# Holding back K matmuls behind the modulation columns, and moving one quarter's scale columns ahead of a chunk's K

## The chip, the cores and the metric

The kernel runs on one core of one Trainium2 chip. The metric is device time in microseconds (us).

## The reference, cut to what matters

```python
x = A_x                                               # (1, 2048, 1024), bf16
mod = (silu(c) @ w_mod).reshape(1, 6, 1, -1)          # w_mod: (1024, 6144)
sa, ca, ga, sb, cb, gb = (mod[:, i] for i in range(6))
h = layernorm(x) * (1 + ca) + sa                      # ca: scale, sa: shift
qkv = h @ A_wqkv                                      # then linear attention with phi(q), phi(k)
x = x + ga * (attention(qkv) @ A_wo)
h = layernorm(x) * (1 + cb) + sb
x = x + gb * ((gelu(h @ B_w_gate) * (h @ B_w_up)) @ B_w_down)
```

Only the start matters here: the scale `1 + ca` and the shift `sa` have to be computed from `c` before any projection of `h` can run.

## The kernel before

Every operation is recorded into one in-order stream for each engine, with semaphore waits worked out from the bytes it reads and writes. TensorE therefore executes its matmuls in the order in which the Python code records them, as the timelines below show.

The first stage works on the first four chunks (128 rows each) of x. A chunk is normalized, transposed on TensorE, copied to `h1T` by ScalarE, and scaled and shifted there by VectorE. The 1024 channels are eight blocks `dc` of 128. A "quarter" q covers `dc` 2q and 2q+1: its modulation values come from 32 small matmuls with one column each, 16 for the shift (`t=0`) and 16 for the scale (`t=1`). VectorE copies them out of PSUM, then scales `h1T`, and only then the K matmuls on these blocks may run.

```python
def wmq_dma(q, ts=(0, 1)):                  # weights of one quarter's columns: shift half first
    for t in ts:
        sch.dma(Q, ... WMQ[q][:, :, t, :] <- w_mod ...)
...
x_dma(0, 1); x_dma(1, 2)
wmq_dma(0, (1,))                            # first quarter: scale half first
x_dma(2, 3)
wmq_dma(0, (0,))
x_dma(3, 4)
w_dma(WK, OFF_WK, "wk", 1, 0, D, 0, 2)      # K weights of dc 0, 1
for q in range(1, 4):
    wmq_dma(q)
    ...                                     # K weights of dc 2q, 2q+1
...                                         # wv, x chunks 4 to 7, wq
```

```python
def mod_cols(q, bank):                      # 32 matmuls 128x1
    for t in range(2):
        for b in range(2):
            for dc in range(NDC): ...       # waits for r_wmq(q, t)

def k_part(q, cs):                          # K matmuls of quarter q for the chunks cs
    for dc in (2 * q, 2 * q + 1):
        for (c_, jg), b in kb0.items():     # seven PSUM banks; chunk 3's second half has bank 4
            if c_ in cs:
                kv_mm(c_, "k", jg, b, [dc])
        if 3 in cs:
            k31([dc])
```

`warm(n)` records n matmuls on zeros, to keep TensorE busy while it would wait. The order of the first stage is in the diff below. After it come V of the four chunks, then the rest of the kernel.

Of the kernel before, what the change touches and what calls it, by code (L numbers as in the profile page):

```python
# [17 lines left out]
NDC = D // P  # L18
# [196 lines left out]
def bass_adaLN_cond__linear_attn_block__geglu_ffn__prompt_kernel(  # L215
# [15 lines left out]
    with ExitStack() as es:  # L231
# [85 lines left out]
        def r_sm(name):  # L317
            return [(SMO[name], SMO[name] + SMSZ[name], name)]
# [13 lines left out]
        def r_h1(sg, k0=0, k1=NDC, s0=0, s1=SGW):  # L332
            return r_t8(H1O[sg], f"h1T{sg}", k0, k1, s0, s1)
# [7 lines left out]
        def r_w(off, name, dc, c0=0, c1=D):  # L341
            return [(off + (dc * D + c0) * 2, off + (dc * D + c1) * 2, name)]
# [14 lines left out]
        def r_wmq(i, t):  # L357
            return [(MSO[i] + (dc * 2 + t) * 512, MSO[i] + (dc * 2 + t + 1) * 512, f"wmq{i}") for dc in range(NDC)]
# [33 lines left out]
        def pr(b):  # L392
            return [(b * 2048, (b + 1) * 2048)]

        def PS(b, c0=0, c1=512):
            return ps_all[:, b * 512 + c0: b * 512 + c1]
# [17 lines left out]
        def pset_writer(b, o):  # L414
            for t_ in pr(b):
                sch.ps.set_writer(t_[0], t_[1], o)
# [87 lines left out]
        def xhat_dve(c_, dst, rng):  # L504
            sch.op(V, lambda e: e.tensor_scalar(dst[:, :], XALL[:, c_, :], MVA[:, c_, 0:1], RSA[:, c_:c_ + 1],
                                                op0=ALU.subtract, op1=ALU.mult),
                   rd=r_x(c_) + r_smc("mv", c_, 8) + r_smc("rs", c_, 4), wr=rng, note=f"xhat {c_}")
# [21 lines left out]
        def xh_buf(c_):  # L529
            i = c_ % 3  # L530
            return XH[i], r_2k(XHO[i], f"xh{i}")
# [52 lines left out]
        def mod1(c0, n, dc0=0, dc1=NDC):  # L584
            sg, ci = divmod(c0, CPG)
            mods(H1, r_h1, sg, sc1, ci * P, (ci + n) * P, dc0, dc1, "h1")
# [5 lines left out]

        MC0 = 496

        def mod_cols(q, bank):
            o = None
            rng = [(bank * 2048 + (MC0 + q * 4) * 4, bank * 2048 + (MC0 + q * 4 + 4) * 4)]
            for t in range(2):
                for b in range(2):
                    col = MC0 + q * 4 + t * 2 + b  # L600
                    for dc in range(NDC):
                        o = sch.op(T, lambda e, t=t, b=b, dc=dc, col=col: e.matmul(  # L602
                            PS(bank, col, col + 1), WMQ[q][:, dc, t, b * P:(b + 1) * P], SILUT[:, dc:dc + 1],
                            start=(q == t == b == dc == 0), stop=(dc == NDC - 1), skip_group_check=True),
                            rd=r_wmq(q, t) + r_sm("siluT"), pwr=(rng if dc == 0 else ()), note=f"mod{q}.{t}.{b}.{dc}")
            for t_ in rng:
                sch.ps.set_writer(t_[0], t_[1], o)

        def mod_copy(q, bank):
            rng = [(bank * 2048 + (MC0 + q * 4) * 4, bank * 2048 + (MC0 + q * 4 + 4) * 4)]  # L610
            sch.op(V, lambda e: e.tensor_tensor(MODT[:, q * 4:q * 4 + 4], PS(bank, MC0 + q * 4, MC0 + q * 4 + 4), ADD4[:, :], ALU.add),
                   prd=rng, rd=r_sm("add4"), wr=r_smc("modt", q, 16), note=f"modcp{q}")
# [62 lines left out]
        def kv_mm(c_, kind, jg, bank, dcs):  # L675
            sg, ci = divmod(c_, CPG)
            W_, off, name = (WK, OFF_WK, "wk") if kind == "k" else (WV, OFF_WV, "wv")
            o = None
            for dc in dcs:
                o = sch.op(T, lambda e, dc=dc: e.matmul(PS(bank), H1[sg][:, dc, ci * P:(ci + 1) * P], W_[:, dc, jg * 512:(jg + 1) * 512],  # L680
                                                        start=(dc == 0), stop=(dc == NDC - 1)),
                           rd=r_h1(sg, dc, dc + 1, ci * P, (ci + 1) * P) + r_w(off, name, dc, jg * 512, (jg + 1) * 512),
                           pwr=(pr(bank) if dc == 0 else ()), note=f"{kind} c{c_} jg{jg} dc{dc}")
            if dcs[-1] == NDC - 1:
                pset_writer(bank, o)
# [26 lines left out]
        def nb():  # L712
            b = bank_i[0] % bank_i[1]
            bank_i[0] += 1
            return b
# [18 lines left out]
        def warm(n, bank=None):  # L734
            for _ in range(n):
                sch.op(T, lambda e: e.matmul(PS(0 if bank is None else bank), WARM[:, 0:P], WARM[:, :], start=bank is not None,
                                             stop=bank is not None, skip_group_check=True),
                       rd=R_WARM, pwr=pr(bank) if bank is not None else (), note="warm")
# [12 lines left out]
        kb0 = {(0, 0): 0, (0, 1): 1, (1, 0): 2, (1, 1): 3, (2, 0): 5, (2, 1): 6, (3, 0): 7}  # L751

        def k31(dcs, c0=0, c1=MC0):
            rng = [(4 * 2048 + c0 * 4, 4 * 2048 + c1 * 4)]
            for dc in dcs:
                o = sch.op(T, lambda e, dc=dc: e.matmul(PS(4, c0, c1), H1[0][:, dc, 3 * P:4 * P], WK[:, dc, 512 + c0:512 + c1],  # L756
                                                        start=(c0 > 0 and dc == 0), stop=(dc == NDC - 1), skip_group_check=True),
                           rd=r_h1(0, dc, dc + 1, 3 * P, 4 * P) + r_w(OFF_WK, "wk", dc, 512 + c0, 512 + c1),
                           pwr=(rng if dc == 0 else ()), note=f"k c3 jg1 dc{dc} {c0}")
            if dcs[-1] == NDC - 1:  # L760
                sch.ps.set_writer(*rng[0], o)

        def k_part(q, cs):
            for dc in (2 * q, 2 * q + 1):
                for (c_, jg), b in kb0.items():
# [4 lines that stand above are left out]
# [10 lines left out]
        ln1_fin(1)  # L780
        warm(6, 7)
        mod_cols(0, 4)
        ln1_bn(2, 0)
        xhat_dve(1, *xh_buf(1))
# [4 lines left out]
        mod1(0, 1, 0, 2)  # L789
        warm(4, 7)  # L790
        k_part(0, [0])
        xhat_dve(2, *xh_buf(2))
        t1(2, 7)
        mod1(1, 1, 0, 2)
        ln1_bn(3, 0)
        ln1_bn(3, 1)
        ln1_fin(3)
        k_part(0, [1])
        mod1(2, 1, 0, 2)
        warm(2)  # L800
        k_part(0, [2])
        xhat_dve(3, *xh_buf(3))
        mod_cols(1, 4)
        mod_copy(1, 4)
        t1(3, 7)
        mod1(0, 3, 2, 4)
        k_part(1, [0, 1, 2])
        mod1(3, 1, 0, 4)
        k_part(0, [3])
        k_part(1, [3])  # L810
        mod_cols(2, 4)
        mod_copy(2, 4)
        warm(2)
        mod1(0, 1, 4, 5)
        mod1(1, 3, 4, 5)
        mod1(0, 4, 5, 6)
        k_part(2, [0, 1, 2])
        mod_cols(3, 4)
        mod_copy(3, 4)
        mod1(0, 1, 6, 8)  # L820
        mod1(1, 3, 6, 8)
        for dc in (4, 5):
            kv_mm(3, "k", 0, kb0[3, 0], [dc])
        for (c_, jg), b in kb0.items():
            kv_mm(c_, "k", jg, b, [6, 7])
        k31([4, 5, 6, 7])
# [4 lines left out]
        for c_ in range(4):  # L831
            for vc, jg in (((0, 0), (1, 0)), ((0, 1), (1, 1)), ((2, 0), (2, 1)), ((3, 0), (3, 1)))[c_]:
                b = nb()
# [58 lines left out]
        for c_ in range(4, NCH):  # L892
# [23 lines left out]
            for jg in range(2):  # L916
                b = nb()
# [3 lines left out]
            for jg in range(2):  # L921
                b = nb()
# [386 lines left out]
```

## Time and profile before

| | before |
|---|---|
| time, median of the first 3 runs | 838.55 us (838.42 to 838.92) |
| span of the profiled run | 836.7 us |
| TensorE busy | 830.1 us, 99% |
| TensorE's waits in the first 70 us | 4.2 us |
| first V matmul starts | 31.53 us |

First, from the page of the kernel before, the busy time of each engine and the chain of work that ended last. TensorE is the limit nearly everywhere.

```profile
PE 830.1 (99%) x4194; PEld 384.4 (46%) x4194; DVE 512.2 (61%) x898; ACT 336.4 (40%) x555; POOL 37.4 (4%) x91
PE 98%; DMA 1%; DVE 0%; SPq 0%; ACT 0%; issue 0%
```

The list of who waited for whom (TensorE, first 70 us): how long in total, how many times, the longest. L478 is the transpose of c, L602 the modulation columns, L680 the K and V matmuls, L565 VectorE's scaling of h1T; further down, L546 is the transposes of a chunk and L756 the K matmuls of chunk 3's second half.

```profile
PE ps_all L478 <- DMA c<-in_c_dram: 2.4, 1, 2.4
PE ps_all L602 <- DMA wmq<-in_w_mod_dram: 1.1, 1, 1.1
PE ps_all L680 <- DVE h1T L565: 0.7, 4, 0.2
```

The four short waits understate what is lost there, because warm-up matmuls (L736) fill part of each. This is seen in the timeline of TensorE, kernel before. Its columns are start, length to the end of the last instruction's pipeline, what, and in brackets the idle time before it and what ended it.

```profile
13.33 1.03 PE L680 MATMUL ps_all<-wk,h1T 128*128 128x512 bf16 x4
14.20 0.59 PE L736 MATMUL ps_all<-warm 128*128 128x512 bf16 x2
14.96 1.04 PE L680 MATMUL ps_all<-wk,h1T 128*128 128x512 bf16 x4 [0.17 <-DVE h1T L565]
15.84 0.94 PE L602 MATMUL ps_all<-siluT,wmq 128*128 128x1 bf16 x32
...
21.75 0.94 PE L602 MATMUL ps_all<-siluT,wmq 128*128 128x1 bf16 x32
22.55 0.59 PE L736 MATMUL ps_all<-warm 128*128 128x512 bf16 x2
23.30 2.76 PE L680 MATMUL ps_all<-wk,h1T 128*128 128x512 bf16 x12 [0.15 <-DVE h1T L565]
25.90 0.94 PE L602 MATMUL ps_all<-siluT,wmq 128*128 128x1 bf16 x32
26.70 0.59 PE L680 MATMUL ps_all<-wk,h1T 128*128 128x512 bf16 x2
27.45 3.20 PE L680 MATMUL ps_all<-wk,h1T 128*128 128x512 bf16 x14 [0.15 <-DVE h1T L565]
30.49 1.18 PE L756 MATMUL ps_all<-wk,h1T 128*128 128x496 bf16 x12
31.53 0.59 PE L680 MATMUL ps_all<-wv,h1T 128*128 128x512 bf16 x2
```

Start to start, the 12 K matmuls from 23.30 to 25.90 take 2.60 us, 0.216 us each; 32 columns take 0.80 us, 0.025 us each. The stretches that end at 14.96, 23.30 and 27.45 us are the targets of the change. From 22.55 to 23.30 us nothing useful ran (0.75 us); from 26.70 to 27.45 us two K matmuls did.

A reading that no printed line gives: the time at which a transfer landed. A transfer raises its semaphore in 16 steps, and the trace records the time of each. The Trainium skill, page "DMA: Bandwidth & Descriptors", section "Why a DMA increments its semaphore by 16 and not by 1", says that up to 16 engines finish independently and that only the full 16 means that all data landed. The second quarter's scale half, in the kernel before: its sixteenth step came at 15.46 us. All landing times below are sixteenth steps. The shift half, issued before it, landed at 13.68 us.

### The profile page before, as it was taken

What the parts mean: (1) busy time and instruction counts of PE and PEld (TensorE: products, weight loads), DVE (VectorE), ACT (ScalarE), POOL (GpSimd) and SP (SyncE); (2) the same over time, 40 slices, a digit from 0 to 9 for tenths busy, and PEclk for the clock granted to TensorE, in tenths of its full rate; (3) what the DMA queues carried; (4) which work ended last, traced back from release to release, by engine and by line L of the source; (5) the groups of instructions that cost most, each with busy time, mean ns of one, the idle gap of its engine ahead of it and who ended that gap; (6) DMA issues with size and microseconds to landing.
All of it is one profiled execution on the core that took longest, in us unless ns stands there. A gap on an engine that the chain in (4) does not pass through costs nothing.

```text
span 836.7 us, 11362 instructions
## 1 busy us (share of the span) xinstructions
PE 830.1 (99%) x4194; PEld 384.4 (46%) x4194; DVE 512.2 (61%) x898; ACT 336.4 (40%) x555; POOL 37.4 (4%) x91
## 2 busy tenths in 40 slices
PE   8999999999999999999999999999999999999998
PEld 4444444444444444444444444444444444444445
DVE  6678877687785577753455665356556535655512
ACT  2357777446423355420354442045554104445300
POOL 2012111000200000010000000000000000000000
DMA  9984422239696779180555533055553305555000
GB/s 288 318 250 104 99 76 76 77 80 235 139 237 203 225 203 275 29 194 26 158 151 151 152 101 76 19 158 152 151 151 101 76 20 159 153 154 144 7 19 26
DMA packets 184102, 113.22 MB, mean 135 GB/s; under 512 B 35560, under 2 KB 175080, under 8 KB 183024
## 3 DMA queue, kind: packets, MB, share of 16 engines
q1 hardware_dynamic: 184032, 112.50, 49.8%
q8 instruction: 33, 0.54, 0.3%
q14 instruction: 21, 0.17, 0.1%
q10 hardware_dynamic: 16, 0.00, 0.0%
HBM read 100.67 MB, written 4.47 MB: 126 GB/s over the span
## 4 chain that ended last, share of the span: by engine, by line
PE 98%; DMA 1%; DVE 0%; SPq 0%; ACT 0%; issue 0%
PE ps_all L1149 23%; PE ps_all L1121 23%; PE ps_all L1124 23%; PE ps_all L680 13%; PE ps_all L1064 7%; PE ps_all L721 7%; PE ps_all L702 1%; DMA wmq<-in_w_mod_dram 1%; PE ps_all L966 0%; PE ps_all L602 0%; PE ps_all L978 0%; PE ps_all L756 0%; PE ps_all L643 0%; SPq L442 0%; DVE h1T L565 0%; ACT h1T L548 0%
## 5 line engine op out<-in xcount | busy, mean ns | idle before, releaser
L1121 PE MATMUL ps_all<-h2T,wg 128*128 128x512 bf16 x896 | 339.6, 379 | 0.0
L1124 PE MATMUL ps_all<-h2T,wu 128*128 128x512 bf16 x896 | 339.6, 379 | 0.0
L1149 PE MATMUL ps_all<-wd,yT 128*128 128x512 bf16 (+3 forms) x952 | 194.2, 366 | 0.0
L1132 ACT ACTIVATE q<-ps_all 128x512 f32<-128x512 f32 x112 | 66.9, 597 | 225.3 <-PE ps_all L1121 221.5
L1149 PEld LDWEIGHTS ps_all<-wd,yT 128*128 128x128 bf16 x952 | 90.1, 98 | 103.9 <-issue 0.4
L1121 PEld LDWEIGHTS ps_all<-h2T,wg 128*128 128x128 bf16 x896 | 87.7, 98 | 105.8 <-issue 0.2
L1124 PEld LDWEIGHTS ps_all<-h2T,wu 128*128 128x128 bf16 x896 | 87.7, 98 | 105.6
L1137 DVE SCALAR_TENSOR_TENSOR ww<-th,guh 128x512 f32<-128x512 f32 x112 | 77.5, 692 | 77.9 <-ACT th L1136 77.9
L1134 DVE SCALAR_TENSOR_TENSOR ww<-q,ps_all 128x512 f32<-128x512 f32 x112 | 76.9, 687 | 77.5 <-ACT guh L1133 77.5
L1136 ACT ACTIVATE th<-ww 128x512 f32<-128x512 f32 x112 | 70.5, 629 | 87.4 <-DVE ww L1134 87.4
L1154 DVE TENSOR_TENSOR ps_all<-ps_all,gbb 128x512 f32<-128x512 f32 (+3 forms) x34 | 22.7, 667 | 94.8 <-PE ps_all L1149 94.8
L1139 DVE TENSOR_TENSOR yT<-ww,ps_all 128x512 bf16<-128x512 f32 x112 | 76.9, 686 | 3.8
L1133 ACT ACTIVATE guh<-ps_all 128x512 f32<-128x512 f32 x112 | 66.2, 591 | 0.0
L721 PE MATMUL ps_all<-h1T,wq 128*128 128x512 bf16 x256 | 58.7, 379 | 0.0
L680 PE MATMUL ps_all<-wk,h1T 128*128 128x512 bf16 x248 | 57.2, 379 | 0.7 <-DVE h1T L565 0.7
L680 PE MATMUL ps_all<-wv,h1T 128*128 128x512 bf16 x256 | 57.7, 379 | 0.0
L669 ACT ACTIVATE eb<-ps_all 128x512 f32<-128x512 f32 x64 | 37.5, 599 | 49.4 <-PE ps_all L721 21.8
L1064 PE MATMUL ps_all<-w,pq 128*128 128x512 bf16 x256 | 56.2, 379 | 0.0
L670 DVE TENSOR_SCALAR eb<-eb 128x512 f32<-128x512 f32 x64 | 27.1, 423 | 26.0 <-ACT eb L669 25.7
L1064 PEld LDWEIGHTS ps_all<-w,pq 128*128 128x128 bf16 x256 | 25.0, 98 | 30.2 <-issue 0.2
L680 PEld LDWEIGHTS ps_all<-wv,h1T 128*128 128x128 bf16 x256 | 24.9, 98 | 29.5
L680 PEld LDWEIGHTS ps_all<-wk,h1T 128*128 128x128 bf16 x248 | 23.7, 98 | 30.1 <-DVE h1T L565 2.9
(96 smaller groups left out, 481.7 us busy)
## 6 DMA issues: line engine op xcount, KB each, us to landing
wg<-in_B_w_gate_dram SPq DMA_DIRECT2D x56, 512.0 KB, 4.1
wu<-in_B_w_up_dram SPq DMA_DIRECT2D x56, 512.0 KB, 5.3
rb<-scr_rd SPq DMA_DIRECT2D x32, 256.0 KB, 6.7
wd<-in_B_w_down_dram SPq DMA_DIRECT2D x7, 1024.0 KB, 9.3
wmst<-in_w_mod_dram SPq DMA_DIRECT2D x6, 1024.0 KB, 6.9
wmq<-in_w_mod_dram SPq DMA_DIRECT2D x8, 512.0 KB, 6.9
out_dram<-xall SPq DMA_DIRECT2D x31, 128.0 KB, 1.7
xall<-in_A_x_dram SPq DMA_DIRECT2D x3, 1024.0 KB, 12.2
```

The lines of the kernel that those rows point to most:

```text
L680: o = sch.op(T, lambda e, dc=dc: e.matmul(PS(bank), H1[sg][:, dc, ci * P:(ci + 1) * P], W_[:, dc, jg * 512:(jg + 1) * 512], start=(dc == 0 ...
L721: o = sch.op(T, lambda e, dc=dc: e.matmul(PS(b), WQ[:, dc, qc * P:(qc + 1) * P], H1[sg][:, dc, :], start=(dc == 0), stop=(dc == NDC - 1)), ...
L1064: last[half] = sch.op(T, lambda e, g=g, half=half: e.matmul(PS(b0 + half), PQ[sg][:, g, ci * P:(ci + 1) * P], W2[:, g, half * 512:(half + ...
L1121: og = sch.op(T, lambda e, dc=dc: e.matmul(PS(bg), WG[slot][:, dc, e_ * P:(e_ + 1) * P], H2[sg][:, dc, :], start=(dc == 0), stop=(dc == ND ...
L1124: ou = sch.op(T, lambda e, dc=dc: e.matmul(PS(bu), WU[slot][:, dc, e_ * P:(e_ + 1) * P], H2[sg][:, dc, :], start=(dc == 0), stop=(dc == ND ...
L1132: sch.op(A, lambda e: e.activation(Q1[j][:, :], PS(bg), ACTF.Square, scale=math.sqrt(GELU_A)), prd=pr(bg), wr=rq, note=f"q1 {fc}")
L1133: ogh = sch.op(A, lambda e: e.activation(GUH[j][:, :], PS(bg), ACTF.Copy, scale=0.5), prd=pr(bg), wr=rg, note=f"gh {fc}")
L1134: sch.op(V, lambda e: e.scalar_tensor_tensor(WW[j][:, :], Q1[j][:, :], 1.0, PS(bg), op0=ALU.add, op1=ALU.mult), rd=rq, prd=pr(bg), wr=rw, ...
L1136: sch.op(A, lambda e: e.activation(TH[j][:, :], WW[j][:, :], ACTF.Tanh, scale=GELU_C), rd=rw, wr=rt, note=f"th {fc}")
L1137: sch.op(V, lambda e: e.scalar_tensor_tensor(WW[j][:, :], TH[j][:, :], 1.0, GUH[j][:, :], op0=ALU.add, op1=ALU.mult), rd=rt + rg, wr=rw, n ...
L1139: sch.op(V, lambda e: e.tensor_tensor(YT[:, fc, :], WW[j][:, :], PS(bu), ALU.mult), rd=rw, prd=pr(bu), wr=r_yt(fc), note=f"yT {fc}")
L1149: o = sch.op(T, lambda e, b=b, fc=fc, c0=c0, c1=c1, n=n: e.matmul(PS(b, 0, n), YT[:, fc, ci * P:(ci + 1) * P], WDT[fc // 4][:, fc % 4, c0:c1],
```

## The change

Its intent: fill the stretches in which TensorE waits for VectorE with real work. Four K matmuls of chunks 2 and 3 are held back and recorded behind the third quarter's columns, and four (two more than before) behind the fourth's. For the second quarter the 16 scale columns go ahead of chunk 2's K, in place of a warm-up pair. Columns now run scale first by default, in every quarter; the order of the transfers is not changed.

```diff
--- before.py
+++ after.py
@@ -592,16 +592,16 @@
 
         MC0 = 496
 
-        def mod_cols(q, bank):
+        def mod_cols(q, bank, ts=(1, 0)):
             o = None
             rng = [(bank * 2048 + (MC0 + q * 4) * 4, bank * 2048 + (MC0 + q * 4 + 4) * 4)]
-            for t in range(2):
+            for t in ts:
                 for b in range(2):
                     col = MC0 + q * 4 + t * 2 + b
                     for dc in range(NDC):
                         o = sch.op(T, lambda e, t=t, b=b, dc=dc, col=col: e.matmul(
                             PS(bank, col, col + 1), WMQ[q][:, dc, t, b * P:(b + 1) * P], SILUT[:, dc:dc + 1],
-                            start=(q == t == b == dc == 0), stop=(dc == NDC - 1), skip_group_check=True),
+                            start=(q == b == dc == 0 and t == 1), stop=(dc == NDC - 1), skip_group_check=True),
                             rd=r_wmq(q, t) + r_sm("siluT"), pwr=(rng if dc == 0 else ()), note=f"mod{q}.{t}.{b}.{dc}")
             for t_ in rng:
                 sch.ps.set_writer(t_[0], t_[1], o)
@@ -759,6 +759,11 @@
                            pwr=(rng if dc == 0 else ()), note=f"k c3 jg1 dc{dc} {c0}")
             if dcs[-1] == NDC - 1:
                 sch.ps.set_writer(*rng[0], o)
+
+        def k_tiles(dcs, tiles):
+            for dc in dcs:
+                for c_, jg in tiles:
+                    kv_mm(c_, "k", jg, kb0[c_, jg], [dc])
 
         def k_part(q, cs):
             for dc in (2 * q, 2 * q + 1):
@@ -797,30 +802,33 @@
         ln1_fin(3)
         k_part(0, [1])
         mod1(2, 1, 0, 2)
-        warm(2)
+        mod_cols(1, 4, (1,))
         k_part(0, [2])
         xhat_dve(3, *xh_buf(3))
-        mod_cols(1, 4)
+        mod_cols(1, 4, (0,))
         mod_copy(1, 4)
         t1(3, 7)
         mod1(0, 3, 2, 4)
-        k_part(1, [0, 1, 2])
+        k_tiles([2, 3], [(0, 0), (0, 1), (1, 0), (1, 1)])
+        k_tiles([2], [(2, 0), (2, 1)])
         mod1(3, 1, 0, 4)
         k_part(0, [3])
-        k_part(1, [3])
+        k31([2, 3])
         mod_cols(2, 4)
         mod_copy(2, 4)
-        warm(2)
+        k_tiles([3], [(2, 0), (2, 1)])
+        k_tiles([2, 3], [(3, 0)])
         mod1(0, 1, 4, 5)
         mod1(1, 3, 4, 5)
         mod1(0, 4, 5, 6)
-        k_part(2, [0, 1, 2])
+        k_tiles([4, 5], [(0, 0), (0, 1), (1, 0), (1, 1)])
+        k_tiles([4], [(2, 0), (2, 1)])
         mod_cols(3, 4)
         mod_copy(3, 4)
         mod1(0, 1, 6, 8)
         mod1(1, 3, 6, 8)
-        for dc in (4, 5):
-            kv_mm(3, "k", 0, kb0[3, 0], [dc])
+        k_tiles([5], [(2, 0), (2, 1)])
+        k_tiles([4, 5], [(3, 0)])
         for (c_, jg), b in kb0.items():
             kv_mm(c_, "k", jg, b, [6, 7])
         k31([4, 5, 6, 7])
```

## The prediction

> **What bounds the kernel now.** The page gives a span of 836.7 us with TensorE busy 99%; the chain of waits runs 98% through TensorE. Its waits in the list lie in the first 28 us: 2.4 us for c, 1.1 us for the first modulation weights, four of 0.15 to 0.20 us for VectorE's h1T scaling. From the last K block at 27.45 us on, the timeline shows matmuls without a gap, so what the first V matmul (31.53 us) gains, the span gains, if later transfers are in time.
>
> **Durations in the trace.** A 128x512 matmul issues every 0.216 us, a modulation column matmul every 0.025 us (32 take 0.80 us). The Trainium skill, page "TensorE: Matmul & The Clock Gate", section "Wait — 56ns, not 53.3ns?", states N/2.4 + 2.5 ns and a floor near 25 ns; the trace agrees. After a quarter's columns VectorE takes a copy (0.16 us) and a scaling (0.31 to 0.38 us) before the next K matmul: 0.75 to 0.81 us on TensorE.
>
> **What the change does, on the chain.**
> - Warm-up: two pairs go (0.43 us each). Each only filled a wait; alone that gains nothing.
> - Third quarter: before, 22.55 to 23.30 us (0.75 us) held no useful matmul. Now four held-back K matmuls (0.86 us) fill it: gain 0.75 us.
> - Fourth quarter: 26.70 to 27.45 us held two K matmuls (0.43 us); now four: gain 0.32 us.
> - First quarter, scale columns first: those weights landed at 6.3 us, so 16 columns run before the shift weights land (9.80 us): 0.40 us earlier. But the first K block needs wk's first part, landed at 11.89 us by its semaphore's increments, and K started at 12.03: the gain is lost there.
> - Second quarter: the scale columns move from 15.8 us to 14.2 us, ahead of chunk 2's K. The queue loads the shift half first (landed 13.68 us), the scale half second: 15.46 us by its last increment. TensorE takes its work in order, so it stalls from 14.2 to about 15.5 us, when chunk 2's K could have run at 14.96. Then 16 columns (0.40), four K (0.87), 16 columns (0.40) end at about 17.2 us against 16.64: cost 0.54 us.
>
> Later transfers are in time by this count: wk 2-3 16.86 (needed 18.0), third quarter's columns 20.40 (21.4), fourth's 24.60 (25.25), wk 7 25.99 (26.9), wv 27.67 (31.0).
>
> **Sum** (an estimate from these durations): +0.54 - 0.75 - 0.32 = about -0.5 us.
>
> **Prediction:** 838.0 us; 8 in 10 between 837.2 and 838.7. Faster by over 2%: 0.003; within 2%: 0.994; slower by over 2%: 0.003.
>
> **What the profile should show.** A new TensorE wait of about 1.3 us for wmq near 14.2 us; chunk 2's K near 15.9 us rather than 14.96; the first V near 31.0 us; the 0.15 us waits behind the third and fourth quarters' columns gone; the first K still near 12.0 us; everything after 31 us as before, some 0.5 us earlier; wmq and wk landing as before.
>
> **What would make it wrong.** If the scale half lands by 14.2 us in unprofiled runs, the cost vanishes and up to 1.1 us is gained, limited then by the fourth quarter's columns at 24.60 us. If transfers land later, or the idle stretch lowers the TensorE clock, the gain shrinks or becomes a loss. If the span does not follow the first V matmul, some later transfer or VectorE work binds at a fixed time. Noise of a few tenths of a us is of the effect's own size.

## The result, and the profile after

| | before | after |
|---|---|---|
| median | 839.04 us (6 runs, 838.42 to 840.65) | 838.45 us (6 runs, 838.12 to 839.1) |
| ratio of fast runs, 95% interval | | 0.9992 [0.9979, 1.0005] |
| span of the profiled run | 836.7 us | 836.2 us |
| first V matmul starts | 31.53 us | 31.00 us |
| from there to the end | 805.21 us | 805.22 us |

A ratio is the mean time of one kernel's fast runs over that of the other's of the same rounds, so it is not quite the ratio of the medians. The interval includes 1: these times alone do not show this change. (Pooled with the round of after_again below, 15 runs of before have a mean of 838.98 us and 11 of the change 838.49 us, 0.49 us apart; their ranges overlap.) Where time is gained and lost is read from the traces. From the first V matmul to the end it is 805.21 or 805.22 us in all thirteen profiled executions, whatever the kernel, so the start of the first V matmul carries the whole difference between them.

The list of TensorE's waits after the change, first 70 us:

```profile
PE ps_all L478 <- POOL bmask L429: 2.1, 1, 2.1
PE ps_all L602 <- DMA wmq<-in_w_mod_dram: 1.9, 2, 1.0
PE ps_all L680 <- DMA wk<-in_A_wqkv_dram: 0.4, 1, 0.4
PE ps_all L680 <- DVE h1T L565: 0.2, 1, 0.2
```

Three of the four waits for VectorE's scaling are gone, and a second wait for `wmq`, of 1.0 us, is new. The timeline of TensorE after the change shows both:

```profile
13.52 1.03 PE L680 MATMUL ps_all<-wk,h1T 128*128 128x512 bf16 x4
15.52 0.55 PE L602 MATMUL ps_all<-siluT,wmq 128*128 128x1 bf16 x16 [0.98 <-DMA wmq<-in_w_mod_dram]
15.94 1.02 PE L680 MATMUL ps_all<-wk,h1T 128*128 128x512 bf16 x4
16.80 0.54 PE L602 MATMUL ps_all<-siluT,wmq 128*128 128x1 bf16 x16
...
21.45 0.94 PE L602 MATMUL ps_all<-siluT,wmq 128*128 128x1 bf16 x32
22.25 3.18 PE L680 MATMUL ps_all<-wk,h1T 128*128 128x512 bf16 x14
25.27 0.94 PE L602 MATMUL ps_all<-siluT,wmq 128*128 128x1 bf16 x32
26.08 4.04 PE L680 MATMUL ps_all<-wk,h1T 128*128 128x512 bf16 x18
29.96 1.19 PE L756 MATMUL ps_all<-wk,h1T 128*128 128x496 bf16 x12
31.00 1.02 PE L680 MATMUL ps_all<-wv,h1T 128*128 128x512 bf16 x4
```

Behind the third and fourth quarter's columns K now runs on without a gap (14 and 18 matmuls in a row). Where the warm-up pair was, TensorE stands still until 15.52 us: the four K matmuls from 13.52 us, 0.216 us each, filled the time to 14.38. The chain of work after the change puts a transfer at that place:

```profile
7.17 8.31 DMA wmq<-in_w_mod_dram
15.48 0.05 issue
15.52 0.55 PE ps_all L602 x16
16.08 0.89 PE ps_all L680 x4
```

The transfer ends at 15.48 us, the sixteenth step of the scale half; the shift half had landed at 13.84 us. Chunk 2's first scaled block was ready at 15.09 us on VectorE, and its weights had landed at 12.07 us, so its K could have run about 0.8 us before it did.

### The profile page after: what moved, and what is told of

It is laid out like the page before. It is cut to its first block, busy times and chain, and to the rows that moved or that the text cites. A ratio compares the mean times of both kernels' runs of the same rounds, so it can differ in the third digit from the quotient of the medians.

```text
span 836.2 us, 11354 instructions
## 1 busy us (share of the span) xinstructions
PE 829.1 (99%) x4190; PEld 384.3 (46%) x4190; DVE 512.3 (61%) x898; ACT 336.3 (40%) x555; POOL 37.5 (4%) x91
## 4 chain that ended last, share of the span: by engine, by line
PE 98%; DMA 1%; SPq 1%; DVE 0%; issue 0%
PE ps_all L1157 23%; PE ps_all L1132 23%; PE ps_all L1129 23%; PE ps_all L680 13%; PE ps_all L1072 7%; PE ps_all L721 7%; DMA wmq<-in_w_mod_dram 1%; PE ps_all L702 1%; SPq L442 0%; PE ps_all L974 0%; PE ps_all L602 0%; PE ps_all L986 0%; PE ps_all L756 0%; SPq L453 0%; PE ps_all L643 0%
```

## The experiments

The theory: (a) the held-back K fills the two later stretches, worth about 1.07 us; (b) the early scale columns wait for weights that the queue loads second, which costs about 0.54 us; (c) the first quarter's order and the warm-up pairs are worth nothing. Rivals: splitting the columns costs by itself; the gain comes from the warm-up pairs or the first quarter; the transfers limit the stage altogether, so that a removed wait returns elsewhere.

How to read them. The landing of one and the same transfer moves by up to 1.6 us between executions (wk's first part, 11.28 to 12.88 us in the eleven traces that load it at the same place). The first K starts 0.13 to 0.14 us behind that landing in most traces. So the first V alone does not compare two kernels: before, e5 and e6 all took 19.50 or 19.51 us from the first K to the first V, but had the first V at 31.53, 31.80 and 31.09 us. Both the first V and the distance from the first K to it are given. The readings of all profiled executions, in us:

| kernel | wk's first part landed | first K | chunk 2's K | first V | first K to first V |
|---|---|---|---|---|---|
| before | 11.89 | 12.03 | 14.96 | 31.53 | 19.50 |
| after | 12.07 | 12.21 | 15.94 | 31.00 | 18.79 |
| e1_shift_first | 11.55 | 11.69 | 14.62 | 30.93 | 19.24 |
| e2_scale_loaded_first | 12.88 | 13.02 | 15.96 | 31.03 | 18.01 |
| e3_hold_back_only | 12.22 | 12.36 | 15.29 | 31.02 | 18.66 |
| e4_scale_early_only | 12.33 | 12.46 | 16.22 | 32.37 | 19.91 |
| e2_again | 12.32 | 12.46 | 15.39 | 31.26 | 18.80 |
| e5_first_quarter_scale_first | 12.16 | 12.29 | 15.23 | 31.80 | 19.51 |
| e6_no_warm_pairs | 11.45 | 11.59 | 14.52 | 31.09 | 19.50 |
| e7_best | 11.02 | 11.45 | 14.39 | 30.84 | 19.39 |
| after_again | 11.28 | 11.41 | 15.30 | 30.88 | 19.47 |
| e1_again | 12.13 | 12.27 | 15.20 | 30.45 | 18.18 |
| e7_again | 10.65 | 11.03 | 13.97 | 30.13 | 19.10 |

All kernels gave correct results. The profiled runs are of the fast state, except those of e5 and e6, which ran once and have the state unknown; the granted clock was 1.00 in all.

### e1_shift_first and e1_again: the other half of the columns first

```diff
 # in the changed kernel
-        mod_cols(1, 4, (1,))
+        mod_cols(1, 4, (0,))
         k_part(0, [2])
         xhat_dve(3, *xh_buf(3))
-        mod_cols(1, 4, (0,))
+        mod_cols(1, 4, (1,))
```

> The changed kernel with one edit: of the second quarter's columns the shift half, whose weights land first (13.7 us), goes ahead of chunk 2's K, and the scale half behind it. If the 1.0 us wait at 14.5 us is the landing of the scale half's weights at 15.48 us (theory), it goes: the early columns run at 14.4, chunk 2's K start near 15.1 us on VectorE's scaling, the scale columns near 16.0, and the first V matmul comes at 30.3 us instead of 31.0 (before: 31.53); 0.7 us less than the change, 1.2 us less than before, ratio to before 0.9985. The fourth quarter's columns then come up against their landing at 24.5 us, a wait of at most 0.1 us. If splitting the columns around K is itself what costs (rival), the first V matmul stays at 31.0 us.

Measured: 837.92 us (5 runs, 837.74 to 838.44), ratio to before 0.9988 [0.9975, 1.0]. The early columns ran at 13.86 us (planned about 14.4; this execution's first K was half a us earlier), without a wait. But the first V came at 30.93 us, not 30.3. The timeline of TensorE in this run shows where the gain went:

```profile
20.99 0.95 PE L602 MATMUL ps_all<-siluT,wmq 128*128 128x1 bf16 x32 [0.68 <-DMA wmq<-in_w_mod_dram]
21.81 3.18 PE L680 MATMUL ps_all<-wk,h1T 128*128 128x512 bf16 x14
25.20 0.95 PE L602 MATMUL ps_all<-siluT,wmq 128*128 128x1 bf16 x32 [0.20 <-DMA wmq<-in_w_mod_dram]
```

TensorE now reached the third quarter's columns before their scale half, which landed at 20.95 us in this execution (20.40 and 20.31 in before and after). The fourth quarter's landed at 25.15 us (24.60 and 24.47). So part of the time saved turned into waits for later transfers, which the expectation allowed for 0.1 us at most. To see whether this belonged to the execution, the same kernel ran again, together with the changed kernel.

> The version with only the second quarter's two column halves swapped, on the same chip as the changed kernel. Theory: no wait at the early columns, and the gain partly given back where the third and fourth quarter's weights land late; median time 0.2 to 0.8 us below the changed kernel's. Rival (the transfers are the limit altogether, and removing the stall only moves the wait): within 0.15 us of the changed kernel.

Measured: 838.35 us (5 runs, 837.8 to 839.01), ratio 0.9996 [0.9982, 1.0009]. In this trace the third and fourth quarter's weights landed at 20.40 and 24.66 us, and the profile lists no wait for `wmq` behind the first quarter. Only the fourth quarter's columns came 0.16 us behind the slots of the 14 K matmuls before them (24.71 us), right behind their landing:

```profile
14.44 0.54 PE L602 MATMUL ps_all<-siluT,wmq 128*128 128x1 bf16 x16
15.20 1.04 PE L680 MATMUL ps_all<-wk,h1T 128*128 128x512 bf16 x4 [0.23 <-DVE h1T L565]
16.08 0.54 PE L602 MATMUL ps_all<-siluT,wmq 128*128 128x1 bf16 x16
...
24.71 0.95 PE L602 MATMUL ps_all<-siluT,wmq 128*128 128x1 bf16 x32
...
30.45 1.67 PE L680 MATMUL ps_all<-wv,h1T 128*128 128x512 bf16 x7
```

With wk's first part landing at 12.13 us, near the 12.07 of the changed kernel, the first V came at 30.45 against 31.00 us: first K to first V took 18.18 against 18.79 us. That shows the stall's cost against the version without it (0.6 us) and refutes the rival that the split costs by itself. In time, however, the median was only 0.17 us below the changed kernel's (838.52 on the same chip), less than the 0.2 expected and close to what the third rival expects; with ranges that overlap, the times do not tell.

### e2_scale_loaded_first and e2_again: the same program, two transfers swapped

```diff
 # in the changed kernel
-            wmq_dma(q)
+            wmq_dma(q, (1, 0) if q == 1 else (0, 1))
```

> The changed kernel with its program for the engines as it is, and only the two transfers of the second quarter's columns issued in the other order, scale half first. Theory: the scale half lands near 13.7 us and the shift half near 15.5, the wait before the early columns is gone and the first V matmul comes at 30.3 us, as with the columns swapped. Rival (the split, or the order of the columns, costs by itself): the first V matmul stays at 31.0 us although the landings change.

Measured: 838.39 us (5 runs, 837.68 to 839.4), ratio 0.9993 [0.998, 1.0007]. The scale half, now loaded first, landed at 14.49 us and the shift half at 16.13 us, and the stall in front of the early columns is gone although no engine's order of work changed, only the queue's:

```profile
13.02 1.02 PE L680 MATMUL ps_all<-wk,h1T 128*128 128x512 bf16 x4 [1.17 <-DMA wk<-in_A_wqkv_dram]
13.88 0.61 PE L546 MATMUL ps_all<-ident,xh 128*128 128x128 bf16 x8
14.33 1.03 PE L680 MATMUL ps_all<-wk,h1T 128*128 128x512 bf16 x4
15.19 0.54 PE L602 MATMUL ps_all<-siluT,wmq 128*128 128x1 bf16 x16
15.96 1.04 PE L680 MATMUL ps_all<-wk,h1T 128*128 128x512 bf16 x4 [0.22 <-DVE h1T L565]
```

The first V was expected at 30.3 us and came at 31.03, a miss in absolute terms: in this execution wk's first part landed at 12.88 us, latest of all, and the whole stage began late. Counted from the first K, the first V came after 18.01 us instead of the changed kernel's 18.79. So the loading order is the cause of the stall; whether the swap also delays wk's first part was open, and the kernel ran again.

> The kernel with the second quarter's two transfers swapped, unchanged, looked at again, because its profiled execution had the first part of wk land at 12.88 us (11.55 to 12.33 in the others) and the first V matmul at 31.03 us where 30.3 was expected. If the late landing was that execution's own, the first part of wk now lands at 11.5 to 12.4 us and the first V matmul comes 18.0 us after the first K matmul, at 29.8 to 30.5 us. If swapping the two later transfers delays wk's first part, it lands at 12.8 us or later again.

Measured: 838.55 us (5 runs, 837.88 to 839.37), ratio 0.9996 [0.9983, 1.0008]. wk's first part landed at 12.32 us, within the range expected for "that execution's own". The early columns again had no wait. But first K to first V took 18.80 us, not 18.0: waits of 0.23 and 0.21 us for `wmq` stood before the third and fourth quarter's columns, whose weights landed at 21.27 and 25.47 us. The loss at 14 us is gone and a late landing gives it back further on, as in e1_shift_first.

### e3_hold_back_only

```diff
 # in the kernel before: the k_tiles edits of the change alone
-        k_part(1, [0, 1, 2])
+        k_tiles([2, 3], [(0, 0), (0, 1), (1, 0), (1, 1)])
+        k_tiles([2], [(2, 0), (2, 1)])
...
-        warm(2)                        # the second pair, behind mod_copy(2, 4)
+        k_tiles([3], [(2, 0), (2, 1)])
+        k_tiles([2, 3], [(3, 0)])
...                                     # k_part(1, [3]) -> k31([2, 3]); the fourth quarter as in the diff
```

> The kernel before with the held-back K matmuls alone (which takes away the second warm-up pair); first and second quarter's columns as before, first warm-up pair kept. Theory: the two waits behind the third and fourth quarters' columns are filled, 0.75 + 0.32 us, so the first V matmul comes at 30.5 us (before 31.53, change 31.0), ratio to before about 0.9987; the fourth quarter's columns would start at 24.7 us, just behind their landing. Rival (the gain of the change comes from the first quarter's order and the warm-up pairs taken away, not from holding back): the first V matmul stays near 31.5 us.

Measured: 837.92 us (5 runs, 837.83 to 838.4), ratio 0.9988 [0.9975, 1.0]; first K to first V 18.66 us, 0.84 us less than before (1.07 expected), first V at 31.02 us (30.5 expected). The parts: chunk 2's K to the third quarter's columns fell from 6.79 to 5.93 us (the four K held back), third to fourth quarter's columns from 4.15 to 3.82 us, as expected (0.8 of columns and 14 K at 0.216). The last part, fourth quarter's columns to the first V, took 5.98 us where 5.73 was due (as in the change, 25.27 to 31.00): wk's last part landed at 27.04 us in this execution (25.99 in before), and the K that needed it started at 27.18 us, 0.47 us behind the K before it instead of 0.22. So the mechanism is as expected, the gain belongs to holding back, and a late transfer took 0.25 us of it. Part (a) of the theory holds without anything of the other edits.

### e4_scale_early_only

```diff
 # in the kernel before
-        warm(2)
+        mod_cols(1, 4, (1,))
         k_part(0, [2])
         xhat_dve(3, *xh_buf(3))
-        mod_cols(1, 4)
+        mod_cols(1, 4, (0,))
```

> The kernel before with the second quarter's scale columns moved ahead of chunk 2's K alone, in place of the first warm-up pair; nothing held back. Theory: TensorE waits for the scale half's landing near 15.5 us and chunk 2's K start near 15.9, so the first V matmul comes at 32.05 to 32.1 us, 0.54 us later than before (31.53); ratio to before about 1.0006. Rival (removing the warm-up pair pays for the split): 31.5 us or less.

Measured: 839.43 us (5 runs, 838.64 to 839.77), ratio 1.0003 [0.9991, 1.0016]. The wait stands where the change put it:

```profile
15.81 0.55 PE L602 MATMUL ps_all<-siluT,wmq 128*128 128x1 bf16 x16 [1.01 <-DMA wmq<-in_w_mod_dram]
16.22 1.02 PE L680 MATMUL ps_all<-wk,h1T 128*128 128x512 bf16 x4
```

The scale half landed at 15.76 us, 0.30 us later than the 15.46 the expectation was built on, and the first V came at 32.37 us, 0.30 us later than the 32.07 expected. This part of the change alone is a loss in the trace: 0.41 us counted from the first K. It is too small for the times to show.

### e5_first_quarter_scale_first

```diff
 # in the kernel before
-        mod_cols(0, 4)
+        mod_cols(0, 4, (1, 0))         # and the start flag on the first one executed
```

> The kernel before with the first quarter's scale columns ahead of its shift columns alone. Theory: the columns end some 0.4 us earlier than the landing of the shift half plus 0.8 us, but the first K matmul still starts 0.1 to 0.15 us behind the landing of wk's first part, with a wait for that transfer showing; from the first K to the first V it takes 19.5 us as before. The first V matmul moves by no more than that landing does. Rival (the first quarter's columns hold the first K block): the first K starts 0.4 us earlier than in before with wk landing the same.

839.17 us, first K to first V 19.51 us against 19.50. Half of the columns ran early, but the first K gained nothing:

```profile
8.52 0.54 PE L602 MATMUL ps_all<-siluT,wmq 128*128 128x1 bf16 x16
9.73 0.55 PE L602 MATMUL ps_all<-siluT,wmq 128*128 128x1 bf16 x16 [0.67 <-DMA wmq<-in_w_mod_dram]
...
12.29 1.02 PE L680 MATMUL ps_all<-wk,h1T 128*128 128x512 bf16 x4 [0.68 <-DVE h1T L565]
```

The line names VectorE as what ended the last wait, yet VectorE's first scaling ended at 10.91 us. The transfer of wk's first part landed at 12.16 us, 0.13 us before the K. A wait for several semaphores is put down to one of them; where that one had long been done, look for another, here a DMA.

### e6_no_warm_pairs

```diff
 # in the kernel before, in two places
-        warm(2)
```

> The kernel before without the two warm-up pairs that the change removes, nothing else. Theory: each pair only filled a wait for VectorE, so from the first K to the first V matmul it takes 19.5 us as in before, and the waits for h1T grow by the 0.43 us of each pair (to about 0.6 us); granted clock 1.00, matmuls still every 0.216 us. Rival (the pairs delay real work): 18.6 to 19.1 us from first K to first V.

838.45 us, first K to first V 19.50 us, the same as before; matmuls still 0.216 us apart and the granted clock 1.00. The waits grew by what the pairs had filled (list of TensorE's waits, and its timeline):

```profile
PE ps_all L680 <- DVE h1T L565: 1.6, 4, 0.6
```

```profile
14.52 1.04 PE L680 MATMUL ps_all<-wk,h1T 128*128 128x512 bf16 x4 [0.60 <-DVE h1T L565]
```

So the pairs cost nothing and removing them gains nothing.

### e7_best, after_again and e7_again: a version without the stall, beside the change

```diff
 # in the changed kernel
-        x_dma(3, 4)
         w_dma(WK, OFF_WK, "wk", 1, 0, D, 0, 2)
+        x_dma(3, 4)
...                                     # second quarter as in e1_shift_first
-        mod_cols(2, 4)
+        mod_cols(2, 4, (0, 1))
...
-        mod_cols(3, 4)
+        mod_cols(3, 4, (0, 1))
```

Each quarter's columns run in the order in which their weights are loaded, so that only 16 columns, not 32, stand behind the later landing; and wk's first part, which holds the first K, is loaded before chunk 3 of x.

> The changed kernel with the shift columns of the second, third and fourth quarter ahead of their scale columns (the order in which their weights are loaded), the second quarter's scale columns behind chunk 2's K, and wk's first part issued ahead of chunk 3 of x. Theory: wk's first part lands near 11.2 us and the first K starts at 11.3 to 11.7 us; no stall before the second quarter's early columns; the first V matmul comes at 29.9 us where the transfers land as in before, up to 30.6 us where they land late; ratio to before about 0.998. If instead the transfers as a whole are the limit, the waits gained at the start come back as waits for the third and fourth quarter's weights and wk's last part, and the first V matmul stays at 30.3 to 30.9 us as in the kernel with the columns swapped.

Measured: 838.15 us (5 runs, 837.18 to 838.25), ratio 0.9986 [0.9973, 1.0]. wk's first part landed at 11.02 us and the first K came at 11.45 us. The first V came at 30.84 us, outside the 29.9 to 30.6 us of the theory and inside the 30.3 to 30.9 us expected if the transfers are the limit: waits of 0.47 and 0.24 us for the third and fourth quarter's scale half, which landed late in this execution (21.24 and 25.45 us). Then the three versions ran together on one chip.

> The changed kernel itself, timed beside the two versions without its stall on one chip, because the landings moved by several tenths of a us between executions. Theory: from the first K to the first V matmul 18.8 us again, with a wait of 0.7 to 1.3 us for the second quarter's scale weights; first V at 30.8 to 31.5 us; median time 838.2 to 838.8 us, 0.3 to 0.7 us below before.

> The version with all later shift columns first and wk's first part loaded ahead of chunk 3 of x, on the same chip. Theory: median 0.3 to 1.0 us below the changed kernel's, 0.9 to 1.5 us below before; waits for the third quarter's scale weights (0 to 0.5 us) and the fourth's (0 to 0.3 us) are what is left.

Measured, with e1_again, 5 runs each against 9 of before (838.95 us, 838.38 to 839.28):

| | median us | lowest to highest | ratio to before |
|---|---|---|---|
| after_again | 838.52 | 838.25 to 838.72 | 0.9995 [0.9982, 1.0007] |
| e1_again | 838.35 | 837.8 to 839.01 | 0.9996 [0.9982, 1.0009] |
| e7_again | 837.51 | 837.21 to 838.03 | 0.9984 [0.9972, 0.9997] |

The changed kernel's expectation missed in one number: 19.47 us from first K to first V, not 18.8. Its stall was longer (1.14 us), since the first K came early at 11.41 us while the scale half landed at 14.84; and a further wait appeared:

```profile
14.88 0.55 PE L602 MATMUL ps_all<-siluT,wmq 128*128 128x1 bf16 x16 [1.14 <-DMA wmq<-in_w_mod_dram]
...
25.14 0.95 PE L602 MATMUL ps_all<-siluT,wmq 128*128 128x1 bf16 x32 [0.34 <-DMA wmq<-in_w_mod_dram]
```

This means that the distance from the first K is no good measure when the stage is held at a later landing; e7, which starts K early, shows the same. The version e7 had its first V at 30.13 us, with waits of 0.16 and 0.23 us left before the scale columns of the third and fourth quarter. A further wait is hidden: the second quarter's K, at 16.47 us, is listed with 0.46 us for VectorE, but that scaling had ended at 16.16 us, and wk's second part landed at 16.33 us (in e7_best 16.86, 16.53 and 16.72 us). So the third rival is right in part: without the stall, TensorE is held at one landing after another. All five of its runs were faster than all five of the changed kernel's, and its interval to before ends below 1: it is the fastest version run, by 0.16% of the time before. Which of its three additions does it was not taken apart.

## Why the prediction was right

- **Total.** Predicted 838.0 us, range 837.2 to 838.7; measured 838.45, inside, and "within 2%" was right. The point was 0.45 us low against the time measured. It had been set 0.55 us below a median of three runs of before, 838.55 us; over six runs, these three among them, before had 839.04. The two medians there differ by 0.6 us, the two traces by 0.53 us at the first V, and -0.5 us was predicted. That these agree so closely is in part luck (see the second quarter).
- **The span follows the first V matmul.** Right, and the firmest point: 805.21 or 805.22 us remain behind it in every trace.
- **Third and fourth quarter, +0.75 and +0.32 us gained.** Right. Both waits are gone in the timeline after the change, and e3 shows the gain without the other edits (0.84 us, and 0.25 us more were taken by one late transfer).
- **Second quarter, 0.54 us lost.** Right in cause; the size depends on the execution. Predicted: stall to about 15.5 us, chunk 2's K at 15.9, second half ends about 17.2; measured 15.52, 15.94 and 17.20 us. So close an agreement is luck: the scale half landed 0.02 us from where it did in the trace of before, while in the other traces with the queue's old order it landed between 14.84 and 15.76 us. Counted from the first K, the second half of the columns ended 4.61 us later in before and 4.99, 5.15 and 5.02 us later in after, after_again and e4: a loss of 0.38, 0.54 and 0.41 us. The wait was 0.98 us and not "about 1.3", for the same landing: the first K had come 0.18 us later in that execution, and the profile counts a wait from the modelled end of the matmuls before it, at 14.54 us, not from their slot. The edit on the engine's side (e1) and the one on the queue's side (e2) both removed it; e4 shows it alone. The Trainium skill's page "DMA: Bandwidth & Descriptors", section "Queues, rings and completion order", says that each DMA engine consumes the descriptors of a queue in ring order; the landings of the second quarter's halves agree: the one issued second came 1.6 to 1.8 us behind the other in all traces.
- **First quarter and warm-up pairs, nothing gained.** Right: e5 (19.51 us) and e6 (19.50 us) against 19.50 us before. In the trace after the change the profile itself names the transfer of wk before the first K.
- **"Later transfers are in time by this count".** Right in the trace after the change, but it does not hold in general: in after_again the fourth quarter's weights landed at 25.09 us and TensorE waited 0.34 us, and in e1, e2_again and e7 other late landings cost 0.2 to 0.7 us. The prediction took the landings of one trace as fixed; they move by as much as the effect. What it named as a risk ("if transfers land later") happened in part of the executions.
- **The idle stretch and the clock.** Nothing was lost: the granted clock stayed 1.00 over a stall of 1 us. The Trainium skill's page "TensorE: Matmul & The Clock Gate", section "What's actually happening", puts the fall to half clock behind an idle window of about 3.4 us; these stalls are shorter and the matmuls behind them stay 0.216 us apart, which agrees; no run here has an idle window long enough to test that figure.

What stays open: why the landings move. Within one transfer of column or K weights the sixteenth step comes 0.2 to 1.8 us behind the twelfth, and in several executions this lag jumps at one transfer and stays for the next. The kept traces offer a candidate for one such jump, which no run tests: in each of the thirteen, one 16 KB packet of the DMA queue that the profile calls "instruction" starts between 16.45 and 18.81 us and takes 1.2 us (median of the data packets: 0.03 us), and in the next transfers to land one more of the 16 steps comes about 1 us late. In e1_shift_first (packet at 17.80 us) it is the last step of the third quarter's scale half, whose lag jumps from 0.71 to 1.64 us, and TensorE waits 0.68 us for it. In e1_again the late step is not the last, and the landing hardly moves. The lags that begin in the first 9 us are not explained by it. Also open is what the stall costs over many runs: e1's ten runs (837.74 to 839.01 us, mean 838.22) and the changed kernel's eleven (838.12 to 839.1, mean 838.49) overlap.

## What to carry to other kernels

When a small piece of work is moved earlier on an in-order engine, look up when its own inputs land, and take the last of the 16 semaphore steps: here one of two halves was ready at 14 us and the change chose the other, which took 0.4 to 0.5 of the 1.07 us that it gained elsewhere. Hold real work back behind the short dependency chains between engines; a filler that only covers a wait can go or stay. Once such waits are gone and the engine runs close behind the transfers, every saving is taken or left by landings that move by as much as the saving, so judge it by instruction positions in several traces, and order both the transfers and their consumers alike.

## What the Trainium skill lacked or had wrong

- Page "TensorE: Matmul & The Clock Gate", section "Back-to-back issue gap": it gives, for a stream of weight load and matmul pairs, 131 ns a matmul at N = 512 and 81 ns at N = 128, and calls 216 ns the isolated gap. In every trace here each matmul has its own weight load, and the spacing is 0.216 us at N = 512 in long streams and 0.055 to 0.056 us at N = 128 in runs of eight (the transposes, 10.67 to 10.72 us in before): the formula that this section calls isolated, in both cases. It is also the one of the section that the prediction cites, so the page disagrees with itself.
- Page "DMA: Bandwidth & Descriptors": it says that the engines of one transfer finish independently, but gives no size for it in a loaded queue. Here, for transfers of 512 KB, the last of 16 shares came 1.7 us behind the first in before (13.76 to 15.46 us) and up to 2.9 us in e2_scale_loaded_first (wk's first part, 10.03 to 12.88 us), while the two halves of the second quarter landed 1.6 to 1.8 us apart.
- The same page says nothing of how far a landing moves between executions: wk's first part, behind the same transfers, landed between 11.28 and 12.88 us in eleven traces, and the time of one kernel spread over 0.5 to 1.7 us in five runs.
